# Scores of the first batch as one float32 product of whole keys and queries, with a new order of operations

## The chip, the core and the metric

The kernel runs on one core of a Trainium2 chip. The core has a matrix engine (TensorE, PE in the profile; its weight loads stand apart as PEld), a vector engine (VectorE, DVE), a scalar engine (ScalarE, ACT), a general engine (GpSimd, POOL) and a queue engine that issues transfers (SyncE, SP). Each works through its own list of instructions in a fixed order, and they wait for each other by semaphores. TensorE reads operands from SBUF and writes only to PSUM, whose eight banks are drained by the other engines. The metric is the device time of one execution in microseconds (us).

## The reference

Three layers follow one another. Four batches of eight heads, 576 positions and 64 numbers a head go through attention in which each query keeps its 32 highest scores; the result goes through a mixture of eight experts with one expert a token; and that through a layer with a softmax-weighted unit and a normalisation.

```python
scores = scale * np.matmul(q, k.transpose(0, 1, 3, 2))
kth = np.partition(scores, -top_k, axis=-1)[..., -top_k:-top_k + 1]   # top_k = 32
scores = np.where(scores >= kth, scores, -1e9)
attn = softmax(scores);  x = attn @ v                 # B, H, S, D = 4, 8, 576, 64
e_idx = np.argmax(x @ w_gate + modality_bias[modality_id], axis=1)
out[e_idx == e] = gate_w * (np.maximum(x @ w1[e], 0) @ w2[e])   # 8 experts, 512 -> 1024 -> 512
h = x @ w_in;  solu = h * softmax(h);  y = layer_norm(solu) * g_ln @ w_out   # 512 -> 1024 -> 512
```

## The kernel before, in words

**Attention.** A batch (b) has four pairs of heads (p) and five tiles of queries (t): four of 128 rows and a last one of 64. `prep_kv` loads the keys of a pair, turns them by TensorE into a PSUM bank and hands them to `parts_of`; `prep_q` does the same for the queries of a tile. `parts_of` (lines 530 to 533) makes two numbers of each float32 number: ScalarE copies the bank into the plane `hi` in the type float32r, which keeps fewer bits (L532), and VectorE takes the difference into the plane `lo` (L533). A pair of keys takes two such steps, one over 512 columns and one over 128; a query tile takes one over 512, the last tile of a batch two over 256.

`scores` (lines 609 to 633) then makes the scores of one tile and one pair, which the text calls a group of scores. It forms the product from three float32r terms, hi with hi, hi with lo and lo with hi, each in two halves of 288 columns, and for a full tile for the two heads of the pair: 3 x 2 x 2 = 12 matmuls (L628). The two heads lie in the two halves of the array's rows (64 rows each). For the last tile the two heads stand side by side in one operand, and a group has 3 x 2 = 6 matmuls over all 128 rows. A batch has 16 groups of 12 and 4 groups of 6.

From each group `unit` takes one head at a time (a unit): ScalarE copies the two halves out of PSUM (L649, L659), VectorE finds the 32nd highest score by rounds of maximum and replacement (L661 to L678), GpSimd and ScalarE mask and take the exponential (L689 to L693). There are 144 units. `pair` multiplies with the values (L722 to L771), and `route` and `place` pick each token's expert and scatter its row to a list in DRAM (L818 to L858).

**Statics.** The weights `w_in` and `w_out` of the last layer come as doubles and are brought into two float32r planes by ScalarE, GpSimd, VectorE (L386 to L390, L470) and TensorE (L408, L443). The first batch's units and this work run at the same time.

**Experts and the last layer.** When enough rows are listed, `front` picks the fullest expert (L915 to L920), gathers its rows (L933) and turns them (L960); `back` multiplies by `w1` (L1025) and `w2` (L1046) in float32; `moe2` runs the last layer (L1067, L1128) in float32r terms. A float32 matmul of the program shows as two matmuls in the trace: L1025 stands there x960 for 480 of the program.

**The order.** Every operation is a step (`Op`) of a generator. The table `ORDER` is a string of digits, one for each step: the digit says which of the generators that are ready goes next. The buffers (`TUNE`) and the priorities (`GET`) decide which generators are ready. So the string, not the chip, fixes the order of the instructions on every engine.

Of the kernel before, what the change touches and what calls it, by code (L numbers as in the profile page):

```python
# [8 lines left out]
F32 = mybir.dt.float32  # L9
# [9 lines left out]
NP = H // 2  # L19
# [20 lines left out]
    "0022556001111111222202334444441115555513333554455556663666440000011233434366666667777555622223377703344441"  # L40
    "1225663226045437747747406244166644451000031111111130400000411333300033442121332155132333044345113544003002"
    "2221556420644464341444401111133622511114446463624461162233636556444412225115552666643315111111814443333332"
    "6675575751944228611434436633667114411111133011114445411122543323522224400445222255336065046005555110432222"
    "2200005561700205223616333333302660022221146007728584472226901553333384557744446661633334115665656213333547"
    "6222677788111425113316778122311145366676522233011100660001230005544112222222225113501133400555600511222467"
    "3311111115525444000113230000230550034434441111111000520002222113355555667335733302112446666553550000388877"
    "7617999894446361111118002455511220050005777444710005350053344992201187472242665111145333133311461114466115"
    "5115688888823662244166661743233223355443434343345352234452222622116010011224443304678776434234311224005511"
    "1112234343320335500044435553226610055671534444521053153536744154224526332222112002244003335255333000002344"
    "4611751160131557833333323436522245334775677676271166114492534763247788222283226233334623225577777766445443"  # L50
    "3666661226222757564126542524655772333043333115055353400042255000400223323000000011154021200042224004443456"
    "78822224811334555258570007301637788822662aa887800653347844785761334521604111100225562266644123333000046551"
    "1160011662242344552772060044034011120001112242112466666601177777665654522756565558856765888403033331133223"
    "2013232224445501133365533446553366001828333378835558803335454572201322621224411111455666163322412221154577"
    "2331301122305533334240113355541224551111110231200332456700543432224677757747418776662661777741365774422545"
    "3313436111022000133232455000111133335689842321434337422667533115511377122222254506411333453666112222245613"
    "4461556663347250132886868954424444442445663316666561111556111777745110433226565116231234002005555554331311"
    "1111144443152244533545545774201000122335444461551111322205300233400001331200134332400002211167880000544440"
    "2427351115453300000001022686622222474748807877112328664441140343345527704500442522666600077826558868990114"
    "5950411555700007556555034220222004455116665771581118882882223444445502266665773225100011111165335455522506"  # L60
    "0000022153231232311333466661102224255664134221115544432422233033555517757000102667788655522111115544127774"
    "4552311111000555777772944664304707225241115866282735311441434334455599033554aa445519a555775589633ab9255989"
    "8266400511166711167353011115001948882555007420344773333115766565576778945636776785157012334799993388942145"
    "5457443333233324656311022244222344003422300400011116614544336115844113393225957556641110500022272554440024"
    "6776225666200117734300100044846781711665333316744411411300172722999a64466977177763333311177859a11b11113354"
    "4488558188991116626227000555142553677677622264405245663362222554223633302220456666661145451111220885772655"
    "8776340846a91446767567755555552711111334455551288544122467133233035536531424250111111333465541100533222511"
    "4456063121332337891884545413355555254454622233622224775663557223337751130511689377454333512442266171455411"
    "22222005550000007654445577722802633725588a2bb01668888748717457559a6699973334556674445997a339a9aa9991155333"
    "3888888955674444555116877179444424541118167111304331221134434344555602344894331312334433455015556651566666"  # L70
    "4522222222215454666342111000231114444006006612301344220011661111104266726634311111311232555464113342884855"
    "56a430115881a811776533122252666645657528311899555583331332831466899998811188bb3377871178787111974553999799"
    "a91572722244469999a66333388544b559966136794444014367676226356566539181115555114377311117222992542433555446"
    "46467464647161333728111116633552223322776655645415111656578444017658744a9999132222244255568343322224445544"
# [165 lines left out]
def attn_moe_solu_kernel(ctx, tc, q, k, v, mid, w_gate, mbias, w1, w2, w_in, w_out, g_ln, out):  # L240
# [1351 lines left out]
    c = 0  # L1592
# [77 lines left out]
```

## Time and profile before

| | |
|---|---|
| three timed runs | 952.91, 955.68, 955.14 us; median 955.14 us |
| profiled execution: its own time, its span | 952.62 us, 950.8 us |
| TensorE busy | 874.6 us |
| VectorE busy | 779.7 us |
| ScalarE, GpSimd busy | 670.9 us, 585.1 us |

The span runs from the first to the last instruction of the profiled execution; 1.8 us of its time lie around it. Busy time adds what an engine executes, without its waits. A matmul's recorded time contains its way through the array, so the spacing of a stream of matmuls is read from the starts in the timeline. A pair of units is under way from about 8 us on; the first expert's products start at 166 us, the last unit's scores end at about 754 us, and from there TensorE runs through the rest of the experts and the last layer.

### The profile page before, as it was taken

The page shows a single profiled execution, that of the slowest core. Times are in us where ns is not written, and L with a number is a line of the kernel's source. Part 1 is how long each engine was busy: PE and PEld are TensorE (multiplying, and loading weights), DVE is VectorE, ACT ScalarE, POOL GpSimd, SP SyncE. Part 2 cuts the span into 40 slices and gives each one's busy share as a digit, 9 for nine tenths or more (in the row PEclk, how much of TensorE's full clock was granted, in tenths as well). Part 3 has the DMA queues.
Part 4 walks back from the last instruction along what each step waited for, and adds up shares of the span by engine and source line. Part 5 has one row for each costly group of instructions (what it writes and reads, how often), then busy time and mean ns, then how long its engine had stood idle before and what let it go on. Part 6 is the DMA issues. An engine that isn't in the chain of part 4 may idle for free.

```text
span 950.8 us, 21544 instructions
## 1 busy us (share of the span) xinstructions
PE 874.6 (92%) x6830; PEld 730.7 (77%) x6830; DVE 779.7 (82%) x2444; ACT 670.9 (71%) x1698; POOL 585.1 (62%) x1352
## 2 busy tenths in 40 slices
PE   5766787989999999999999999999999999999994
PEld 3544455977888888879888888888887988889872
DVE  7998998999999999999999999999999943422320
ACT  3867876878787778878877788788778863633432
POOL 4677856657666767675677677666677666520222
PEclk9888887999999999999999999999999999999998
DMA  6624233444624343455243434443432337624000
GB/s 173 188 67 138 91 89 93 124 115 140 174 79 148 112 137 113 119 157 154 79 137 103 125 90 138 121 123 113 136 96 86 114 107 224 195 89 118 6 23 26
DMA packets 140952, 110.72 MB, mean 116 GB/s; under 512 B 47233, under 2 KB 116893, under 8 KB 140830
## 3 DMA queue, kind: packets, MB, share of 16 engines
q1 hardware_dynamic: 136478, 93.92, 34.4%
q0 software_dynamic: 4352, 15.34, 4.7%
q8 instruction: 56, 0.92, 0.4%
q14 instruction: 66, 0.54, 0.2%
HBM read 97.11 MB, written 12.13 MB: 115 GB/s over the span
## 4 chain that ended last, share of the span: by engine, by line
PE 50%; DVE 14%; POOL 10%; ACT 5%; issue 5%; DMA 2%; POOLq 0%; DVEq 0%; ACTq 0%
PE po L1128 7%; PE ph L1025 7%; PE py L1046 7%; PE ph L1067 6%; PE po L755 5%; PE pS L628 4%; PE pt L722 4%; DVE M L669 3%; POOL e L691 2%; PE py L1346 2%; PE ph L1326 2%; DVE tht L678 2%; DMA xg<-xlist,li 2%; PE pt L960 1%; PE px L765 1%
## 5 line engine op out<-in xcount | busy, mean ns | idle before, releaser
L691 POOL TENSOR_TENSOR e<-ss,e 128x576 f32<-128x576 f32 x144 | 206.3, 1434 | 55.4 <-ACT e L690 52.9
L693 ACT ACTIVATE e<-e,nb 128x576 f32<-128x576 f32 x144 | 112.0, 778 | 25.7 <-POOL e L691 24.7
L669 DVE MATCH_REPLACE8 M<-tops,M 128x288 f32<-128x288 f32 x288 | 127.4, 445 | 0.0
L1025 PE MATMUL ph<-xT,wraw 128*128 128x128 f32 x960 | 126.2, 278 | 1.1 <-DVE M L662 0.5
L1046 PE MATMUL py<-hh,wraw 128*128 128x128 f32 x960 | 125.8, 278 | 1.1 <-ACT hh L1030 1.1
L690 ACT ACTIVATE e<-ss,bt 128x576 f32<-128x576 f32 x144 | 111.5, 778 | 19.4 <-POOL bt L689 19.2
L1025 PEld LDWEIGHTS ph<-xT,wraw 128*128 128x128 f32 x960 | 115.4, 192 | 6.3 <-issue 3.1
L1046 PEld LDWEIGHTS py<-hh,wraw 128*128 128x128 f32 x960 | 115.3, 192 | 5.6 <-issue 2.7
L1128 PE MATMUL po<-wo,lT 128*128 128x512 f32 x432 | 112.0, 404 | 2.6 <-ACT lT L964 2.6
L1067 PE MATMUL ph<-wi,yT 128*128 128x512 f32 x432 | 110.2, 403 | 0.8 <-ACT ss L649 0.7
L755 PE MATMUL po<-eT,vt 128*64 128x128 f32 (+1 forms) x1600 | 104.7, 273 | 5.2 <-DVE qT L533 1.9
L678 DVE MAX8 tht<-M 128x8 f32<-128x576 f32 x144 | 108.1, 754 | 1.2
L628 PE MATMUL pS<-kT,qT 64*128 64x288 f32 (+1 forms) x864 | 94.4, 322 | 10.0 <-DVE xs L776 4.3
L755 PEld LDWEIGHTS po<-eT,vt 128*64 128x64 f32 x1600 | 84.6, 140 | 20.7 <-ACT eT L725 5.8
L1128 PEld LDWEIGHTS po<-wo,lT 128*128 128x128 f32 x432 | 77.6, 188 | 23.8 <-DVE lT L968 3.3
L1067 PEld LDWEIGHTS ph<-wi,yT 128*128 128x128 f32 x432 | 78.3, 188 | 19.8 <-issue 1.6
L628 PEld LDWEIGHTS pS<-kT,qT 64*128 64x128 f32 (+1 forms) x864 | 72.2, 193 | 27.0 <-issue 7.8
L725 ACT ACTIVATE eT<-pt 128x512 f32<-128x512 f32 x144 | 82.0, 597 | 10.4 <-PE pt L722 9.8
L722 PE MATMUL pt<-identr,e 128*128 128x128 f32 x576 | 85.0, 284 | 4.1 <-ACT e L693 1.7
L722 PEld LDWEIGHTS pt<-identr,e 128*128 128x128 f32 x576 | 68.8, 146 | 12.7 <-ACT e L693 3.5
L661 DVE TENSOR_TENSOR M<-pS,ss 128x288 f32<-128x288 f32 x144 | 64.7, 450 | 9.3 <-ACT ss L659 7.2
L689 POOL TENSOR_SCALAR bt<-tht 128x1 f32<-128x1 f32 x144 | 34.0, 236 | 62.2 <-DVE tht L678 51.7
(256 smaller groups left out, 1848.4 us busy)
## 6 DMA issues: line engine op xcount, KB each, us to landing
wraw<-in_moe_w_dram SPq DMA_DIRECT2D x256, 256.0 KB
kr<-in_k_dram SPq DMA_DIRECT2D x32, 128.0 KB
qr<-in_q_dram SPq DMA_DIRECT2D x16, 256.0 KB
raw<-in_moe_w_out_dram SPq DMA_DIRECT2D x8, 512.0 KB
vt<-in_v_dram SPq DMA_DIRECT2D x32, 128.0 KB
raw<-in_moe_w_in_dram SPq DMA_DIRECT2D x8, 512.0 KB
wstage<-da SPq DMA_DIRECT2D x8, 256.0 KB
wc<-wstage SPq DMA_DIRECT2D x8, 256.0 KB
```

Source lines behind the costliest of these rows:

```text
L628: nc.tensor.matmul(bank[s][hf], x[r, a, p, :], kt[r, c, at:at + HALF], start=i == 0, stop=i == 2)
L669: nc.vector.match_replace(out=M, in_to_replace=rounds[r], in_values=M, imm_value=NEG)
L678: t0 = yield Op("DVE", 660, lambda: nc.vector.max(th, W), deps=[t0, tm])
L690: yield Op("ACT", 667, lambda: nc.scalar.activation(e, ss, AF.Relu, bias=bt, scale=-BIG))
L691: yield Op("POOL", 1360, lambda: nc.gpsimd.tensor_tensor(e, ss, e, op=OP.subtract))
L693: yield Op("ACT", 760, lambda: nc.scalar.activation(e, e, AF.Exp, bias=nb, scale=0.125, accum_out=z))
L722: nc.tensor.transpose(pt[:, c, :], ef[:, at:at + 128], ident)
L755: nc.tensor.matmul(po[hs, :n], w, x, start=c == 0, stop=c == 4)
L1025: nc.tensor.matmul(ph[:, :n], w[:, kk * 128:(kk + 1) * 128], x[0][:, kk, :n], start=kk == 0, stop=kk == KD - 1)
L1046: nc.tensor.matmul(py[c // k_][:, c % k_, :], w[:, c * 128:(c + 1) * 128], hs[m], start=m == 0 and c % k_ == 0, stop=m == KF - 1 and c % k ...
L1067: nc.tensor.matmul(ph, y[a][:, kk, :], wi[b][:, kk, i * 512:(i + 1) * 512], start=kk == 0 and j == 0, stop=kk == KD - 1 and j == 2)
L1128: nc.tensor.matmul(po, l[a][:, c, :], wo[b][:, kk, :], start=kk == 0 and j == 0, stop=kk == KF - 1 and j == 2)
```

## The change

Batch 0 alone is computed in another way (`WHOLE = 1`). `parts_of` then makes one ScalarE copy in float32 into the plane `hi`, and the VectorE step into `lo` is not there. `scores` then forms one float32 product of the planes `hi`, in place of three float32r terms: 4 matmuls of the program for a full tile, 2 for the last one, with the same halves and the same rows of the array. Batches 1 to 3 are as before. The table `ORDER` is a new one over its whole length; a line of it stands in the diff.

```diff
 ORDER = (
-    "0022556001111111222202334444441115555513333554455556663666440000011233434366666666777555622223377703344441"
...
+    "0022556101101112343311114444444455554546666035544466624222393352575788846566777557777766669377882222223375"
...
-    def parts_of(hi, lo, pt, n):
-
+    WHOLE = 1
+
+    def parts_of(b, hi, lo, pt, n):
+
+        if b < WHOLE:
+            yield Op("ACT", 55 + n * 833 // 1000, lambda: nc.scalar.activation(hi.bitcast(F32), pt, AF.Copy))
+            return
         yield Op("ACT", 55 + n * 833 // 1000, lambda: nc.scalar.activation(hi, pt, AF.Copy))
         yield Op("DVE", 70 + n * 1042 // 1000, lambda: nc.vector.tensor_tensor(lo, pt, hi.bitcast(F32), op=OP.subtract))
...
         def mm():
-            for i, (a, c) in enumerate(((0, 0), (0, 1), (1, 0))):
+            terms, dt = (((0, 0),), F32) if b < WHOLE else (((0, 0), (0, 1), (1, 0)), F32R)
+            for i, (a, c) in enumerate(terms):
                 for hf in range(2):
                     for s in range(n // 64):
                         r = slice(64 * s, 64 * s + 64) if n == 128 else slice(0, 128)
                         at = 64 * (1 - s) + hf * HALF
-                        nc.tensor.matmul(bank[s][hf], x[r, a, p, :], kt[r, c, at:at + HALF], start=i == 0, stop=i == 2)
+                        nc.tensor.matmul(bank[s][hf], x[r, a, p, :].bitcast(dt), kt[r, c, at:at + HALF].bitcast(dt),
+                                         start=i == 0, stop=i == len(terms) - 1)
```

The lines behind the first part of the diff move by 5 to 7: L533 of before is L538 of the changed kernel, L628 is L634, L661 is L668, L669 is L676, L672 is L679, L915 is L922.

TensorE at the start of the program, before; `kr` and `qr` are raw keys and queries, `pS` the scores, `da` and `dc` pieces of a static weight:

```order
L563 MATMUL pt<-identr,kr 128x128 x4
L570 MATMUL pt<-identr,kr 128x64
L589 MATMUL pt<-identr,qr 128x128 x4
L628 MATMUL pS<-kT,qT 128x288 x12
L350 MATMUL pt<-identr,cs 128x64
L563 MATMUL pt<-identr,kr 128x128 x4
L570 MATMUL pt<-identr,kr 128x64
L589 MATMUL pt<-identr,qr 128x128 x4
L408 MATMUL pw<-da,identr 128x512
L408 MATMUL pw<-dc,identr 128x512
L443 MATMUL pm<-da,onesf 128x512
```

And the same place now:

```order
L568 MATMUL pt<-identr,kr 128x128 x4
L575 MATMUL pt<-identr,kr 128x64
L594 MATMUL pt<-identr,qr 128x128 x4
L350 MATMUL pt<-identr,cs 128x64
L634 MATMUL pS<-kT,qT 128x288 x4
L594 MATMUL pt<-identr,qr 128x128 x4
L568 MATMUL pt<-identr,kr 128x128 x4
L575 MATMUL pt<-identr,kr 128x64
L408 MATMUL pw<-da,identr 128x512
L634 MATMUL pS<-kT,qT 128x288 x4
L408 MATMUL pw<-dc,identr 128x512
```

The second query tile is turned before the second pair's keys, and the second group of scores stands between the pieces of the first static weight, where before it stood behind two static weights.

VectorE from its first instruction of attention, before; `ss` is a unit's copied half, `M` the larger of each two scores, `tops` the maxima found so far:

```order
L533 TENSOR_TENSOR kT<-pt,kT 128x512
L344 COPY iw<-identr 64x4x64 x2
L533 TENSOR_TENSOR kT<-pt,kT 128x2x64
L533 TENSOR_TENSOR qT<-pt,qT 128x512
L661 TENSOR_TENSOR M<-pS,ss 128x288
L662 TENSOR_TENSOR M<-pS,ss 128x288
L665 MAX tops<-M 128x8
L661 TENSOR_TENSOR M<-pS,ss 128x288
L662 TENSOR_TENSOR M<-pS,ss 128x288
L665 MAX tops<-M 128x8
```

And now:

```order
L344 COPY iw<-identr 64x4x64 x2
L668 TENSOR_TENSOR M<-pS,ss 128x288
L669 TENSOR_TENSOR M<-pS,ss 128x288
L672 MAX tops<-M 128x8
L676 MATCH_REPLACE M<-tops,M 128x288
L668 TENSOR_TENSOR M<-pS,ss 128x288
L669 TENSOR_TENSOR M<-pS,ss 128x288
L679 MAX tops<-M 128x8
L672 MAX tops<-M 128x8
```

Three differences of keys and queries are gone from the head of the list, and the first unit's first replacement stands ahead of the second unit.

VectorE around the first pick of an expert, before; `rk`, `pos` and `cq` belong to the routing of the tile ahead of it, `pmx` to the pick, `qT` here is the last query tile of batch 0:

```order
L852 SCALAR_TENSOR_TENSOR rk,pos<-rk,oh 128x8
L853 TENSOR_TENSOR cq<-cq,pc 128x8
L665 MAX tops<-M 128x8
L672 MAX tops<-M 128x8
L669 MATCH_REPLACE M<-tops,M 128x288
L470 TENSOR_TENSOR wo_101<-pw,wo_100 128x512 x2
L669 MATCH_REPLACE M<-tops,M 128x288
L672 MAX abt<-M 128x8
L533 TENSOR_TENSOR qT<-pt,qT 64x4x64 x2
L669 MATCH_REPLACE M<-abt,M 128x288
L672 MAX tops<-M 128x8
L707 RECIPROCAL rz<-z 128x2
```

And now:

```order
L859 SCALAR_TENSOR_TENSOR rk,pos<-rk,oh 128x8
L860 TENSOR_TENSOR cq<-cq,pc 128x8
L676 MATCH_REPLACE M<-tops,M 128x288
L685 MAX tht<-M 128x8
L679 MAX tops<-M 128x8
L714 RECIPROCAL rz<-z 128x2
L676 MATCH_REPLACE M<-tops,M 128x288
L922 MAX pmx<-pend 128x8
```

The two static differences (L470) and the two query differences (L533) are no longer between the routing and the pick. The pick itself was the 306th instruction of VectorE's list and is the 293rd, 13 instructions earlier.

## Rows read from the trace of the kernel before

**Rows 1.** Page, parts 1 and 2: span; TensorE's granted clock in 40 slices.

```profile
span 950.8 us, 21544 instructions
...
PEclk9888887999999999999999999999999999999998
```

**Rows 2.** Windows by stage: stretch, length, busy time (instructions) by engine, clock, DMA share, GB/s.

```profile
0.00:25.00 25.00, 14.68 (x55) 8.36 (x56) 17.52 (x50) 10.21 (x22) 10.71 (x30) 1.00 0.68 175
25.00:125.00 100.00, 70.84 (x391) 43.84 (x389) 94.99 (x247) 76.34 (x175) 77.32 (x96) 0.85 0.37 112
125.00:163.50 38.50, 31.71 (x190) 21.97 (x191) 35.16 (x110) 26.16 (x65) 22.87 (x51) 0.81 0.38 112
163.50:250.00 86.50, 82.81 (x766) 71.41 (x766) 83.56 (x277) 70.58 (x188) 57.69 (x152) 1.00 0.48 134
250.00:750.00 500.00, 490.27 (x4277) 426.87 (x4276) 476.40 (x1554) 398.22 (x1042) 337.92 (x821) 1.00 0.41 119
750.00:900.00 150.00, 148.40 (x1004) 131.18 (x1003) 61.02 (x187) 73.54 (x182) 64.02 (x168) 1.00 0.40 123
```

**Rows 3.** Chain of waits, 100 to 180 us: start, length, engine, tile, line.

```profile
125.87 1.74 PE pS L628 x9
...
133.94 6.37 PE pw L408 x19
...
145.42 0.99 PE pS L628 x12
...
150.40 0.33 DVE qT L533
...
151.16 0.44 DVE qT L533
...
158.62 5.53 DMA xg<-xlist,li
...
166.15 1.98 PE ph L1025 x16
```

**Rows 4.** Line 533 up to 152 us: count, min/median/max ns, first to last start.

```profile
L533 DVE TENSOR_TENSOR kT<-pt,kT x8: 278/482/692, 6.1 to 35.7; 128x512 fp32r<-128x512 f32 x4, 128x128 fp32r<-128x128 f32 x4
L533 DVE TENSOR_TENSOR qT<-pt,qT x6: 397/669/692, 7.9 to 151.2; 128x512 fp32r<-128x512 f32 x4, 64x256 fp32r<-64x256 f32 x2
```

**Rows 5.** Window up to 152 us, line 533 alone: VectorE's busy time.

```profile
0.00:152.00 152.00, 7.06 (x14) 0.89 0.41 119
```

**Rows 6.** Waits of all engines up to 163.5 us: total, times, longest.

```profile
PE pt L563 <- DMA kr<-in_k_dram: 11.1, 3, 4.4
```

**Rows 7.** Line 628 up to 163.5 us: TensorE's score matmuls.

```profile
L628 PE MATMUL pS<-kT,qT x168: 285/394/607, 7.9 to 162.0; 64*128 64x288 f32 x168
```

**Rows 8.** TensorE's timeline, 340 to 375 us: start, length, line, form, count.

```profile
351.99 1.95 PE L1025 MATMUL ph<-xT,wraw 128*128 128x128 f32 x16
353.78 0.41 PE L765 MATMUL px<-iw,oT 128*128 128x144 f32 x2
...
362.73 1.07 PE L628 MATMUL pS<-kT,qT 64*128 64x288 f32 x12
363.73 0.66 PE L722 MATMUL pt<-identr,e 128*128 128x128 f32 x4
...
368.96 1.31 PE L755 MATMUL po<-eT,vt 128*64 128x128 f32 x20
370.20 3.06 PE L1128 MATMUL po<-wo,lT 128*128 128x512 f32 x12
373.10 0.41 PE L765 MATMUL px<-iw,oT 128*128 128x144 f32 x2
```

**Rows 9.** Groups by form: weight loads in float32 (L1025) and float32r (L628).

```profile
L1025 PEld LDWEIGHTS ph<-xT,wraw 128*128 128x128 f32 x960 | 115.4, 192 | 6.3 <-issue 3.1 <-DVE M L662 0.7 <-DVE xs L835 0.6
...
L628 PEld LDWEIGHTS pS<-kT,qT 64*128 64x128 f32 x768 | 58.9, 194 | 26.0 <-issue 7.6 <-ACT eT L725 4.7 <-DVE xs L776 4.5
```

More of the change, by code (lines that the diff above doesn't have):

```diff
@@ L39 @@
 ORDER = (
[L40 to L74, printed above, removed]
@@ new lines @@
+    "8884455266003455331143345688777275881117722422222222275543577778885664427722227773443666666434334477783155"
+    "5555727245122222456555772945577222226688376674744477773366255554833333333355522776378882442399655588686432"
+    "6666423388976133052522035530221330000103315445524220511222113532200225444556666006623700711656302214534422"
+    "6431668301441181114446156333172622322122333386678513118844236344522277377555555332448471111443666677775277"
+    "2352274711113433545457111121234156666882227722221110024420022222204415511133440011453544522050015662112111"
@@ L95 @@
+    "5555255341344446440075061115522224000144000444444322211112222000111202232233112222003335114112001011014220"
+    "0223010110002230221551334454330301344000000033133440301000000000000000000000000000001123330110012222222222"
+    "2333330011222233222220111110110002111300001033222100110200121000111111221111100300000111100111000111112002"
+    "21200000000000"
 )
@@ L565, in prep_kv @@
         yield Op("PE", 440, tr)
-        yield from parts_of(kt[:, 0, 64:576], kt[:, 1, 64:576], pt.rearrange("p c n -> p (c n)"), 512)
+        yield from parts_of(b, kt[:, 0, 64:576], kt[:, 1, 64:576], pt.rearrange("p c n -> p (c n)"), 512)
         yield "put", ("B", 1)
@@ L572, in prep_kv @@
         ends = kt.rearrange("p a (e n) -> p a e n", n=64)[:, :, 0:10:9, :]
-        yield from parts_of(ends[:, 0], ends[:, 1], bc(pl, 2, 1), 128)
+        yield from parts_of(b, ends[:, 0], ends[:, 1], bc(pl, 2, 1), 128)
         yield "put", ("B", 1)
@@ L593, in prep_q @@
         if n == 128:
-            yield from parts_of(x[:, 0], x[:, 1], pt, NP * n)
+            yield from parts_of(b, x[:, 0], x[:, 1], pt, NP * n)
         else:
@@ L602, in prep_q @@
                 r = slice(64 * s, 64 * s + 64)
-                yield from parts_of(x[r, 0, :, r], x[r, 1, :, r], pt[r], NP * n)
+                yield from parts_of(b, x[r, 0, :, r], x[r, 1, :, r], pt[r], NP * n)
         yield "put", ("B", 1)
```

65 lines of the change are left out of this document (45 added, 20 removed).

## The prediction

> **What bounds the kernel now.** I read the windows by stage first [rows 2]. The reader is to see two regimes. From 163.5 to 900 us TensorE is busy 82.81 + 490.27 + 148.40 = 721.5 of 736.5 us, all of it at the full clock: it is the bound, and only 15.0 us are idle. Up to 163.5 us it is busy 14.68 + 70.84 + 31.71 = 117.2 us and idle 46.3, with a granted clock of 0.85 and 0.81 in two of the three windows. VectorE, in contrast, is busy 94.99 + 35.16 = 130.2 of the 138.5 us between 25 and 163.5: it bounds this first stretch. The page's clock row says the same: digits below 9 stand in the first slices and the last one alone [rows 1].
>
> Then I read the chain of waits around the seam [rows 3]. Between 125 and 146 us it runs on TensorE (a group of scores of 1.74 us at the low clock, 6.37 us of static products, another group of 0.99 us). Then it goes through VectorE, where two query differences of L533 (0.33 and 0.44 us) stand on it themselves, to the gather of the first expert's rows (5.53 us) and to the first expert's products at 166.15 us. So the time is, roughly, the moment at which TensorE becomes dense plus the work that is left for it by then. The change can move the moment, through VectorE, and the work, through the products. I costed both, and then asked what the new order may do.
>
> **What VectorE loses.** In batch 0 the differences of L533 go: up to 152 us the line has 8 instructions for keys (four over 512 columns, four over 128) and 6 for queries (four over 512, two over 256) [rows 4], 14 in all, which are the whole of batch 0. Together they keep VectorE busy 7.06 us [rows 5]. All lie ahead of the first gather, in the stretch that VectorE bounds, so the first term is -7.06 us at most. The first pick moves up by 13 instructions in VectorE's list where 14 are removed, so the new order puts hardly any other work in their place.
>
> Not all of it need arrive. The differences of the keys of pairs 2 to 4 start by 35.7 us, while TensorE waits 11.1 us in three waits for the raw keys [rows 6]. Work that is saved in front of an arrival is not saved after it. A difference over 512 columns takes about 0.68 us and one over 128 about 0.28 (the kinds on either side of the median of 482 ns), so three pairs make 2.9 us. Bounds of the loss are 0 and 2.9. I take 1.0, nearer to nothing, because VectorE idles only 5.0 us between 25 and 125 us [rows 2]: it has static weights to convert meanwhile.
>
> ScalarE's copies stay in number and size, and write another type. I cost them at nothing; ScalarE is busy 76.34 of 100 us in the second window [rows 2], which would hide some tenths. The bank of the turned keys is handed back one VectorE step earlier; I count no gain for it.
>
> **What TensorE gains in work.** Before, a full group takes 1.00 us for 12 matmuls (362.73 to 363.73) [rows 8]. The two heads must be running side by side there, in the two halves of the array: a float32r matmul of 512 columns takes 2.90 / 12 = 0.242 us (370.20 to 373.10) [rows 8], which is 0.136 for 288 columns; six pairs at that price make 0.82 us, and 0.18 are left for filling and draining. Twelve in a row would make 1.63.
>
> A float32 matmul is not shown with 64 rows and 288 columns. From the nearest rows: 16 float32 instructions of 128 columns take 1.79 us (351.99 to 353.78), 0.112 each, two for a matmul of the program [rows 8]. For 288 columns that is 0.252, so a group has 8 instructions, in pairs 4 x 0.252 = 1.01, with the 0.18 it is 1.19 us: +0.19. Float32 instructions do run side by side in halves of the array's columns, 20 in 1.24 us (368.96 to 370.20), 0.062 each [rows 8]; halves of the rows have no float32 row. The price lies between 1.01 (+0.01, nothing to fill) and 8 x 0.252 + 0.18 = 2.20 (+1.20, nothing side by side). I take +0.19, since the pairs of L755 and those of L628 both overlap. A group of the last tile has 6 matmuls over all rows, which become 4 instructions: the same passes and the same +0.19.
>
> Where do they fall? Up to 163.5 us there are 168 score matmuls, 14 groups of 12 [rows 7]; the other two full groups and the four of the last tile come in the dense part, which makes 6 x 0.19 = 1.1 us. Of the 14, two stand on the chain: the one at 145 us (+0.19) and the one at 126 us, which ran at the low clock and costs twice that (+0.4). The other twelve, 2.3 us, are covered by TensorE's 46.3 idle us; if that cover failed they would cost those 2.3. The second term is +1.7 us.
>
> The Trainium skill has a rule that speaks against this change. The loads of weights in float32 take 192 ns in the trace (L1025) and those in float32r 194 (L628) [rows 9]: no difference. "TensorE: Matmul & The Clock Gate", section "Weight-path perf modes — Fast Weight Load (FWL) and DoubleRow", says that the fast way of loading weights is off for float32 and makes loads about twice as quick where it is on. By the rule, eight loads at twice the present spacing of 1.00 / 12 us would pace a group at 1.33 us instead of 1.19, an estimate from that page, and the six dense groups and the two on the chain would add about 1.3 us to the sum. By the rows they add nothing, and the sum goes by the rows.
>
> **The order.** Its price has no row. Macroscopically the lists look alike: on TensorE the same transposes of keys and queries open the program, with the second group of scores some entries earlier. What an order can win or lose in the dense part is bounded by its idle 15.0 us there [rows 2]: it can win no more than these, and I take a third, 5 us, as a fair gain, half as much again, 7.5 us, as a fair loss, and 0 as the value.
>
> **The sum.** -7.06 + 1.0 + 1.7 + 0 = -4.4 us. The profiled execution took 952.62 us, 1.8 more than its span of 950.8 [rows 1], and would take 948.2. It stands 2.5 us below the median of the runs shown, 955.14; from the median the same step gives 950.7 us, and that is the forecast.
>
> **The rivals.** *No change.* The end of the first stretch is set by the arrival of keys and by the static products at 134 us, so that only what VectorE saves behind the keys counts: two query differences of about 0.67 and two of about 0.4 us, 2.1. For it speak the 11.1 us of waits for keys and the 20 us of the chain on TensorE [rows 3, 6]; against it, that the static products wait for static weights which VectorE itself converts. It gives -2.1 + 1.7 = -0.4, 954.7 us.
>
> *Slower: the heads' float32 products do not run side by side.* The place is the group of scores, the price +1.20 us for a full one. The two in the dense part give 2.4, the four of the last tile 0.8, that at 145 us 1.2, that at 126 us at the low clock 2.4, together 6.8; of the twelve others' 14.4 us I let a quarter through, 3.6. The sum is -7.06 + 1.0 + 6.8 + 3.6 = +4.3, 959.4 us. It decides once the extra exceeds the 6.1 us that VectorE brings, when some six pairs in ten run one after the other. For it speaks that no row has such a product; against it, both kinds of pairs that do overlap [rows 8].
>
> *Slower: the new order.* Its dense part has half as many waits again: +7.5, so +3.1 and 958.2 us. For it speaks that this table is new over its whole length, and 15.0 idle us in 736.5 are little to start from; against it, that the picks keep their places.
>
> **How the numbers follow.** The forecast has 0.55, no change 0.20, the products 0.10, the order 0.15. What a measurement of this kernel can tell from no change is 0.3%, 2.9 us, so faster means below 952.3 and slower above 958.0. The forecast's own range is 946.5 to 953; 0.48 of its 0.55 lies below 952.3, and 0.05 comes from the lower edge of no change: faster 0.53. The rest of these two, 0.07 and 0.14, with 0.04 from the order's better half, makes no change 0.25. The products and the rest of the order leave 0.22 for slower. The range reaches from a fair gain by the order, 950.7 - 5, to the order's loss: 945.5 to 958.5.
>
> **What would show it.** The first expert's products should start near 161 us instead of 166. VectorE's busy time up to there should fall by about 7 us, with its share unchanged. A full group of batch 0 should take about 1.2 us at the full clock, with its matmuls starting two by two. TensorE's idle time after the seam should stay near 15 us. A group above 1.8 us would speak for the products; a start at 165 us or later for no change; a start at 161 us with more than 20 idle us behind it for the order. An end well below 946 us would say that the order gains, which I do not count on.

## The result and the profile after

The changed kernel took 943.68 us (median of 4 runs, 943.18 to 947.95), against 955.0 us for the kernel before in runs beside it (median of 4, 952.91 to 955.68). The ratio is 0.9895, with a 95% interval of 0.9863 to 0.9927: about 10 us faster. A later measurement of the same two kernels (e4, below) gave 0.9887. The forecast was 950.7 us with a range down to 945.5, so the direction was right, and the gain is more than twice the 4.4 us that the sum had.

The profiled execution is the lowest of the four: 943.18 us, with a span of 941.4. That of the kernel before took 952.62, which is 2.4 below its median. So the two traces differ by 9.4 us.

The windows of the changed kernel, in the stretches of [rows 2]:

```profile
0.00:25.00 25.00, 15.79 (x54) 8.22 (x56) 16.79 (x55) 12.76 (x28) 11.71 (x33) 1.00 0.66 164
25.00:125.00 100.00, 74.32 (x363) 41.25 (x359) 93.28 (x243) 76.86 (x177) 80.43 (x98) 0.83 0.41 118
125.00:163.50 38.50, 32.14 (x213) 22.25 (x212) 36.83 (x114) 27.73 (x71) 22.88 (x53) 0.91 0.37 107
163.50:250.00 86.50, 84.12 (x764) 72.08 (x764) 82.34 (x280) 70.42 (x188) 59.03 (x155) 1.00 0.51 145
250.00:750.00 500.00, 492.68 (x4274) 428.60 (x4271) 476.82 (x1559) 400.48 (x1046) 337.08 (x819) 1.00 0.41 118
750.00:900.00 150.00, 147.52 (x978) 130.72 (x978) 56.55 (x166) 67.55 (x168) 62.95 (x169) 1.00 0.40 121
```

The reader is to see two things. In the third window TensorE executes 213 matmuls instead of 190 at a clock of 0.91 instead of 0.81: the dense part begins inside it, not behind it. And in the three dense windows TensorE is busy 724.3 of 736.5 us, so 12.2 are idle where 15.0 were.

Fixed stretches blur this, because the seam (the first expert's first product) has moved. So here are two windows of each kernel, first of before, then of after: up to the seam, and from the same place near the end on (the transposes and nine first products of the last layer behind the last float32 expert) to the last matmul:

```profile
0.00:166.10 166.10, 119.66 (x661) 76.05 (x661) 150.26 (x413) 115.29 (x267) 112.17 (x182) 0.87 0.41 120
...
900.00:939.20 39.20, 35.84 (x159) 27.10 (x157) 11.06 (x23) 15.17 (x28) 13.60 (x37) 1.00 0.06 21
```

```profile
0.00:160.90 160.90, 119.64 (x604) 69.16 (x604) 144.30 (x400) 115.06 (x267) 112.59 (x179) 0.87 0.44 124
...
893.20:929.60 36.40, 34.58 (x158) 27.05 (x156) 10.34 (x21) 14.71 (x27) 11.70 (x30) 1.00 0.06 23
```

The seam comes 5.2 us earlier. VectorE is busy 5.96 us less up to it, with 13 instructions fewer, and its share hardly changes: 90.5%, then 89.7%. Behind the seam the kernel before needed 773.1 us to its last matmul and the changed one 768.7 (929.6 - 160.9), 4.4 us less. In the last stretch TensorE does the same work (159 and 158 matmuls) in 36.4 us instead of 39.2: it idles 1.8 us in place of 3.4, and is recorded busy 34.58 us in place of 35.84.

The chain of waits of the changed kernel around the seam, the counterpart of [rows 3]:

```profile
121.70 2.22 PE pS L634 x8
...
130.62 4.43 PE pw L408 x14
...
140.31 1.17 PE pS L634 x8
...
146.16 0.17 DVE pmx L922
...
154.30 2.22 PE pS L634 x8
...
161.00 1.98 PE ph L1032 x16
```

The query differences are gone from it, and so is the gather: behind the pick at 146.16 the chain runs through VectorE's and TensorE's own work for the units. A float32 group of scores shows 2.22 us at the low clock (0.50 is granted in those two stretches, 1.2 GHz) and 1.17 at the full one.

### The profile page after: what moved, and what is told of

Read it like the earlier page. It is cut to its first block, busy times and chain, and to the rows that moved or that the text cites. A ratio compares the mean times of both kernels' runs of the same rounds, so it can differ in the third digit from the quotient of the medians.

```text
span 941.4 us, 21332 instructions
## 1 busy us (share of the span) xinstructions
PE 874.4 (93%) x6758; PEld 724.7 (77%) x6758; DVE 771.6 (82%) x2430; ACT 669.4 (71%) x1698; POOL 585.8 (62%) x1352
## 4 chain that ended last, share of the span: by engine, by line
PE 66%; DVE 10%; POOL 8%; ACT 5%; issue 3%; DMA 1%; POOLq 0%; SPq 0%; DVEq 0%; ACTq 0%
PE ph L1074 9%; PE ph L1032 9%; PE py L1053 9%; PE po L1135 7%; PE po L762 7%; PE pS L634 6%; PE pt L729 5%; POOL e L698 3%; DVE M L676 2%; PE py L1353 2%; PE ph L1333 2%; PE px L772 2%; PE pw L408 2%; PE pt L967 2%; DVE tht L685 1%
## 5 line engine op out<-in xcount | busy, mean ns | idle before, releaser
L1053 PE MATMUL py<-hh,wraw 128*128 128x128 f32 x960 | 128.0, 280 | 0.5 <-ACT hh L1037 0.5
L676 DVE MATCH_REPLACE8 M<-tops,M 128x288 f32<-128x288 f32 x288 | 127.3, 445 | 0.0
L700 ACT ACTIVATE e<-e,nb 128x576 f32<-128x576 f32 x144 | 112.1, 778 | 19.9 <-POOL e L698 18.5
L1053 PEld LDWEIGHTS py<-hh,wraw 128*128 128x128 f32 x960 | 117.2, 194 | 5.7 <-issue 3.8
L762 PE MATMUL po<-eT,vt 128*64 128x128 f32 (+1 forms) x1600 | 101.8, 270 | 2.5 <-ACT eT L732 1.5
L634 PE MATMUL pS<-kT,qT 64*128 64x288 f32 (+1 forms) x792 | 95.2, 342 | 6.7 <-DVE xs L783 3.9
L762 PEld LDWEIGHTS po<-eT,vt 128*64 128x64 f32 x1600 | 82.4, 138 | 19.9 <-ACT eT L732 4.7
L732 ACT ACTIVATE eT<-pt 128x512 f32<-128x512 f32 x144 | 82.7, 601 | 14.9 <-PE pt L729 13.4
L634 PEld LDWEIGHTS pS<-kT,qT 64*128 64x128 f32 (+1 forms) x792 | 67.2, 190 | 26.5 <-issue 6.0
L668 DVE TENSOR_TENSOR M<-pS,ss 128x288 f32<-128x288 f32 x144 | 64.8, 450 | 11.8 <-ACT ss L666 10.4
L656 ACT ACTIVATE ss<-pS 128x288 f32<-128x288 f32 x144 | 57.8, 410 | 15.5 <-PE pS L634 13.7
```

Of the source, the lines that this page charges most:

```text
L634: nc.tensor.matmul(bank[s][hf], x[r, a, p, :].bitcast(dt), kt[r, c, at:at + HALF].bitcast(dt), start=i == 0, stop=i == len(terms) - 1)
L676: nc.vector.match_replace(out=M, in_to_replace=rounds[r], in_values=M, imm_value=NEG)
L700: yield Op("ACT", 760, lambda: nc.scalar.activation(e, e, AF.Exp, bias=nb, scale=0.125, accum_out=z))
L762: nc.tensor.matmul(po[hs, :n], w, x, start=c == 0, stop=c == 4)
L1053: nc.tensor.matmul(py[c // k_][:, c % k_, :], w[:, c * 128:(c + 1) * 128], hs[m], start=m == 0 and c % k_ == 0, stop=m == KF - 1 and c % k ...
```

## The experiments

Two things were changed at once: the arithmetic (differences gone, one float32 product) and the table that sets the order. The theory of the prediction was that the arithmetic carries the gain and that the order is worth about nothing; its rival, after the result, that the order carries most of it. To tell them apart, an order was carried over exactly: the sequence in which one table places its steps was recorded, and a table was written that places the steps of the other kernel in the same sequence, with the 14 differences taken out, or put in right behind their ScalarE copies. Unless said otherwise no other step changes its place.

All ratios are to the kernel before, measured beside them (its medians were 955.53, 956.02 and 954.77 us in the three sets of runs). A ratio difference of 0.1% is 0.95 us.

| run | arithmetic | order | median us | ratio, 95% interval |
|---|---|---|---|---|
| e1 | new | old | 953.19 | 0.9974 (0.9958 to 0.9990) |
| e2 | old | new | 948.97 | 0.9919 (0.9888 to 0.9950) |
| e3 | new | new, old from the wide expert (L1333) on | 946.82 | 0.9904 (0.9882 to 0.9927) |
| e4 | new | new (the changed kernel again) | 944.75 | 0.9887 (0.9865 to 0.9909) |
| e5 | new | old up to the seam, then new | 947.99 | 0.9931 (0.9905 to 0.9958) |
| e6 | new | new up to the seam, then old | 947.45 | 0.9915 (0.9894 to 0.9936) |
| e7 | new | new up to about 39 us, then old | 952.81 | 0.9974 (0.9959 to 0.9990) |
| e8 | no differences, three products | old | 950.83 | 0.9949 (0.9933 to 0.9966) |
| e9 | differences kept, float32 product | old | 955.42 | 1.0011 (0.9994 to 1.0028) |
| e10 | no differences, three products | new | 942.83 | 0.9872 (0.9847 to 0.9896) |
| e11 | new | new up to about 99 us, then old | 949.07 | 0.9936 (0.9913 to 0.9958) |
| e12 | new, in batches 0 and 1 | new | 944.33 | 0.9888 (0.9865 to 0.9912) |

### Arithmetic and order apart: e1 to e4

e1 is the changed kernel with a table that keeps the old sequence (the first line of it):

```diff
 ORDER = (
-    "0022556101101112343311114444444455554546666035544466624222393352575788846566777557777766669377882222223375"
+    "0022556001111112220234444441115555513333554455556663666440000123434366666667777555622223377703344441256632"
```

> The new arithmetic of batch 0, with every remaining operation in the order of the kernel before (only the 14 differences are missing from it). Theory A, the order is the part that I mis-sized: the arithmetic alone gives what the sum said, 4 to 6 us, so about 950 us beside 955, the first expert's products near 161 us and TensorE idle about 18 us from there to its end. Theory B, the arithmetic gives everything: 944 us, idle time behind the seam 14 us or less. Theory C, each order fits only its own arithmetic: 953 us or more.

e2 is the kernel before with a table that has the new sequence:

```diff
 ORDER = (
-    "0022556001111111222202334444441115555513333554455556663666440000011233434366666667777555622223377703344441"
+    "0022556101101111223443311114444444455454546666035544466624222233933525757888465667775577777666693377882222"
```

> The arithmetic of the kernel before, with every operation in the order of the changed kernel (each of the 14 differences stands right behind its copy on ScalarE). Theory A: the order alone gives 4 to 6 us, about 950 us beside 955, first expert's products near 166 us, idle behind the seam about 14 us. Theory B: 955 us. Theory C: slower than before, 957 us or more.

e3 is the changed kernel in which the last 4.6% of the steps stand in the old sequence, from the first product of the wide expert on (L1333, 448 columns in float32r; it starts at 818.7 us). e4 is the changed kernel unaltered.

> The changed kernel up to the first matmul of the last large expert (4.6% of the operations are left then), and from there the remaining operations in the order of the kernel before. In the traces the changed kernel gains 2.7 us behind that point. Theory A in its narrow form, the tail's order is worth these: 2 to 3 us slower than the changed kernel. Rival: the tail only follows what the earlier part left, and the time stays within 1 us of the changed kernel.

> The changed kernel itself beside the others on the same chip, as the mark for e1 to e3. By its four runs so far 943 to 948 us, 11 us below before; if the gap to before here were 5 us, what was left unexplained would be scatter between runs and no order.

The new arithmetic in the old order is 0.26% faster than before, 2.5 us. The new order with the old arithmetic is 0.81% faster, 7.7 us. With both it is 1.13%, 10.8 us. So the order is worth 7.7 us with the old arithmetic and 0.87%, 8.3 us, with the new one (e1 to e4; the intervals are far apart). The theory that the order is worth nothing falls. Of the expectations for e1 none holds as written: the time lies where theory C had it, but by C's reason e2 would have been slower than before, and it is 7.7 us faster; theory A had the arithmetic at 4 to 6 us, and it gave 2.5. For e2 and e3 theory A came true (949 us; 2.1 us behind e4 by the medians).

e1 and the changed kernel execute the same work up to the seam, so their traces can say where the order gains there. The window up to the seam of e1, to be read beside that of after above:

```profile
0.00:169.00 169.00, 126.03 (x604) 73.17 (x604) 144.87 (x399) 115.33 (x267) 112.49 (x182) 0.86 0.41 118
```

Both have 604 matmuls, 399 or 400 VectorE instructions of 144.87 or 144.30 us and 267 ScalarE instructions; but e1 arrives 8.1 us later. VectorE idles 24.1 us in e1 and 16.6 after. One pair of traces is not enough here, though: e5 (below) has the same lists as e1 up to the seam and arrives at 166.5. So here are the traces of all kernels but e12, by the order and the differences that they have. The idle time is the start of the first expert's products less VectorE's busy time up to there:

| order up to the seam | differences of batch 0 | traces | first expert's products start, us | VectorE idle up to there, us |
|---|---|---|---|---|
| old | kept | before, e9 | 166.1, 170.0 | 15.8, 18.7 |
| old | gone | e1, e5, e8 | 169.0, 166.5, 165.8 | 24.1, 21.2, 21.9 |
| new to 39 or 99 us, then old | gone | e7, e11 | 167.4, 166.2 | 23.0, 22.2 |
| new | gone | changed, e3, e4, e6, e10 | 160.9, 161.9, 160.6, 163.1, 160.7 | 16.6, 17.8, 16.6, 18.5, 16.8 |
| new | kept | e2 | 167.4 | 14.7 |

Equal lists lie up to 2.5 us apart. Beyond this scatter, with the differences gone, VectorE idles about 5 us less in the new order and the seam comes 5 to 6 us earlier. With the differences kept the traces show no earlier seam in the new order; what of e2's 7.7 us lies ahead of the seam stays open (the trace of before ran 2.4 us below its median, that of e2 1.2 above).

What VectorE waits for up to 160 us (total, times, longest), in e1 and then in the changed kernel:

```profile
DVE M L668 <- ACT ss L666: 11.6, 4, 7.2
DVE rz L714 <- POOL z L713: 2.5, 3, 1.7
DVE dd L386 <- POOL dd L385: 2.5, 4, 1.0
DVE xs L842 <- POOL se L841: 1.2, 1, 1.2
DVE lg L825 <- ACT xs L778: 1.0, 2, 0.7
```

```profile
DVE M L668 <- ACT ss L666: 7.7, 3, 7.1
DVE dd L386 <- POOL dd L385: 2.9, 5, 1.4
```

The wait of 7.1 to 7.2 us is the one for the first scores at all. Before the change, the first differences of keys and queries stood inside this stretch; without them VectorE simply waits for the copied scores. The waits at `rz` (the reciprocals of the softmax's sums), `xs` and `lg` (two steps of the routing), 4.7 us together, are not among those of the changed kernel. They stand in every trace with the differences gone and the old order from 39 us on (e1, e5, e7 and e8: 4.5 to 4.9 us) and in no trace with the new order up to the seam. The second wait for scores is longest in e1. TensorE in e1, from the end of the second tile's transposes (start, length, line, tile, form, count):

```profile
15.23 1.11 PE L594 MATMUL pt<-identr,qr 128*128 128x128 f32 x4
16.40 2.04 PE L408 MATMUL pw<-da,identr 128*128 128x512 f32 x2
...
22.75 1.42 PE L408 MATMUL pw<-dc,identr 128*128 128x512 f32 x1
24.09 2.19 PE L634 MATMUL pS<-kT,qT 64*128 64x288 f32 x8
```

and the same in the changed kernel:

```profile
16.47 2.07 PE L408 MATMUL pw<-da,identr 128*128 128x512 f32 x2
18.47 1.36 PE L634 MATMUL pS<-kT,qT 64*128 64x288 f32 x8
```

In e1 the second group of scores stands behind the two static weights and begins at 24.09; VectorE, which is through with the first group at 22.93, waits 3.83 us for it:

```profile
21.52 1.41 DVE L685 MAX8 tht<-M 128x8 f32<-128x576 f32 x2
26.76 0.46 DVE L668 TENSOR_TENSOR M<-pS,ss 128x288 f32<-128x288 f32 x1 [3.83 <-ACT ss L666]
```

In the changed kernel it begins at 18.47, between them, and this wait is not there. But e5, with the lists of e1, has its second group at 21.98 and waits only 0.76 us (TensorE, then VectorE):

```profile
21.98 1.24 PE L634 MATMUL pS<-kT,qT 64*128 64x288 f32 x8
```

```profile
23.69 0.46 DVE L668 TENSOR_TENSOR M<-pS,ss 128x288 f32<-128x288 f32 x1 [0.76 <-ACT ss L666]
```

In e8, which has the same order with three products, it waits 3.12 us. What the order saves at this place changes from execution to execution, and no single pair of traces prices it.

At the end lies the other piece that can be named. TensorE's last products in the changed kernel and in the kernel before (the times in brackets are idle time and what ended it):

```profile
909.73 2.96 PE L1135 MATMUL po<-wo,lT 128*128 128x512 f32 x12
...
914.36 2.96 PE L1135 MATMUL po<-wo,lT 128*128 128x512 f32 x12
...
918.89 0.66 PE L967 MATMUL pt<-identr,u 128*128 128x128 f32 x4 [1.13 <-DVE u L1091]
919.30 5.85 PE L1135 MATMUL po<-wo,lT 128*128 128x512 f32 x24
...
926.27 3.33 PE L1135 MATMUL po<-wo,lT 128*128 128x512 f32 x12 [0.69 <-ACT lT L971]
```

```profile
921.85 0.66 PE L960 MATMUL pt<-identr,u 128*128 128x128 f32 x4 [0.75 <-DVE u L1084]
923.20 3.32 PE L1128 MATMUL po<-wo,lT 128*128 128x512 f32 x12 [0.69 <-ACT lT L964]
...
928.60 6.13 PE L1128 MATMUL po<-wo,lT 128*128 128x512 f32 x24 [1.21 <-ACT lT L964]
...
935.85 3.33 PE L1128 MATMUL po<-wo,lT 128*128 128x512 f32 x12 [0.69 <-ACT lT L964]
```

In the old order, three of the last output products wait for ScalarE's copy of their turned operand (0.69, 1.21, 0.69 us). In the new one they are spread so that other products stand before two of them, and one wait of 0.69 is left, beside one of 1.13 for VectorE where before had 0.75. TensorE's idle time falls by 1.5 us. The rest of the gain does not show as idle time: twelve products are recorded with 2.96 us in a stream and with 3.32 behind a wait. e3, with the old end, has the waits of before again (0.75, 0.69, 1.20, 0.69) and is 0.17%, 1.6 us, behind the changed kernel. The intervals of e3 and e4 overlap, but the traces are clear about the end. From the start of the wide expert's first product to that of the last product of all pass 113.4 to 114.0 us in the eight kernels with the old end (before, e1, e3, e6, e7, e8, e9, e11) and 110.5 to 110.6 in the six with the new one (changed, e2, e4, e5, e10, e12): the end is worth 2.9 us, with either arithmetic.

### Where the order gains: e5, e6, e7 and e11

Four kernels with the new arithmetic change from one sequence to the other at a place: at the first expert's first product (e5, e6), at the fourth group of scores (e7), at the ninth (e11). The edit is again the table; for e7, against e1, the first two lines, and from the third on all are alike:

```diff
-    "0022556001111112220234444441115555513333554455556663666440000123434366666667777555622223377703344441256632"
-    "2604543774774740624416664445100031111111304000004113333000334421213321551323330443451135440030022221556420"
+    "0022556101101112343311114444444455554546666035544466624222393352575788846566777557777766669377882222223375"
+    "8884455266003455331143345688777275881117722422222222275543577778885664427722221011551445115443022221556420"
```

> New arithmetic; the operations up to the first expert's first product in the order of before, everything behind it in the new order. Theory A, the order gains in two places, the first stretch and behind it: this one has only the second part, 3 to 4.5 us better than the same arithmetic in the old order throughout (953.2), about 949 to 950 us, with TensorE's last product ending some 769 us behind the first expert's as in the changed kernel. Rival, all of the order's gain lies in the first stretch: 952 to 953 us.

> New arithmetic; the new order up to the first expert's first product, the order of before behind it. Theory A: the first expert's products near 161 us as in the changed kernel, and 772 us from there to the last product as in the kernel before: 948 to 949 us. Rival, all in the first stretch: 944 to 945 us. Rival, nothing in the first stretch: 952 to 953 us.

> New arithmetic; the new order only up to the fourth group of scores (about 39 us, 3% of the operations), then the order of before. In the old order with the new arithmetic VectorE waits 3.8 us at 26.8 us for the second group of scores, which stands behind the products of two static weights on TensorE; in the new order it does not wait there. Theory H, this head is what lets the missing differences be worth something: 3 to 4 us better than the old order throughout (953.2), about 949 to 950 us, first expert's products 4 us earlier than its 169.0. Rival, the waits come back later in the stretch: 952 to 953 us.

> New arithmetic; the new order up to the ninth group of scores (about 99 us in the changed kernel, 9% of the operations), then the order of before. The new order up to 39 us alone gave 0.4 us, up to 161 us 5.7 us. Theory, the gain builds up along the stretch, in the pieces where VectorE no longer waits for GpSimd and ScalarE's static weights: 949 to 951 us. Rival, it lies in the last part, the static products and the first pick from 99 to 161 us: 952 to 953 us.

Against e1 (0.9974), the new order up to 39 us brings nothing (e7, 0.9974), up to 99 us 0.38%, 3.6 us (e11), up to the seam 0.59%, 5.6 us (e6). The new order behind the seam alone brings 0.43%, 4.1 us (e5). The intervals of e6 and e1 lie apart; those of e5 and of e11 touch that of e1. The two parts, 5.6 and 4.1, come to 9.7 where the whole order brings 8.3, so within the intervals they add up, and the part behind the seam is worth 2.7 us (8.3 - 5.6) to 4.1. The end's 2.9 us fill this. In the dense part between, from the first expert's products to the wide expert's, the traces show no gain by the order: 656.5 to 659.3 us in the old one, 655.4 to 658.2 in the new one, with TensorE idle 11.8 to 14.9 and 11.4 to 14.4 us.

e11 came where its theory had it, e5 and e6 up to a microsecond below theirs, and e6 started its first expert at 163.1 and not near 161.

e7 was a miss that teaches. It has the second group of scores early and waits 0.74 us for it, against 3.83 in e1 and 0.76 in e5; yet its time is that of e1. VectorE's waits in e7 up to 160 us:

```profile
DVE M L668 <- ACT ss L666: 8.6, 4, 7.0
DVE dd L386 <- POOL dd L385: 4.2, 5, 1.0
DVE rz L714 <- POOL z L713: 2.8, 2, 2.4
DVE xs L842 <- POOL se L841: 1.2, 1, 1.2
DVE lg L825 <- ACT xs L778: 0.9, 2, 0.6
```

The waits at `rz`, `xs` and `lg` are all still there, and VectorE idles 23.0 us up to the seam, as with the old order. In e11 the wait at `rz` is gone and the two others stand. Beside e1, the 3.0 us fewer at the scores stand against 1.7 more for GpSimd's step of the static weights (L385) and 0.3 more at `rz`. GpSimd in turn waits there for ScalarE. Between 38 and 100 us this is 3.9 to 5.0 us in e1, e5 and e8, and 0.2 to 2.0 in the kernels that have the new order to 99 us or farther. The line in e7 and in the changed kernel:

```profile
POOL dd L385 <- ACT dd L383: 7.9, 5, 2.4
```

```profile
POOL dd L385 <- ACT dd L383: 2.0, 2, 1.8
```

So nothing is gained by the head alone, and the gain comes with the orders that go on to place the steps behind it otherwise (e11, e6). That it comes by the static steps, and by the waits at `rz`, `xs` and `lg`, is a reading of traces; no run changed these steps alone.

### The two halves of the arithmetic: e8, e9, e10 and e12

e8 takes the differences away and keeps three float32r products: of the high plane with itself, three times, so that the low parts are left out of batch 0's scores. The order is the old one. e10 is the same in the new order.

```diff
-            yield Op("ACT", 55 + n * 833 // 1000, lambda: nc.scalar.activation(hi.bitcast(F32), pt, AF.Copy))
+            yield Op("ACT", 55 + n * 833 // 1000, lambda: nc.scalar.activation(hi, pt, AF.Copy))
...
-            terms, dt = (((0, 0),), F32) if b < WHOLE else (((0, 0), (0, 1), (1, 0)), F32R)
+            terms, dt = ((0, 0),) * 3 if b < WHOLE else ((0, 0), (0, 1), (1, 0)), F32R
```

> Order of before without the 14 differences; the scores of batch 0 keep three float32r terms, each formed from the high planes, so the low parts are left out of them and TensorE has the work of the kernel before. Theory W, what VectorE saves falls into waits for the keys and the scores: 952 to 954 us, VectorE's idle time up to the first expert's products 6 us or more above the 15.8 of before. Rival P, VectorE's saving arrives and the dearer products of batch 0 eat it: 949 us or less, seam 6 us earlier than in the kernel before.

> New order, without the differences, batch 0's scores as three float32r terms of the high planes (the low parts are left out of them). Beside the old arithmetic in the new order (949.0) it lacks only VectorE's 7 us; beside the changed kernel (944.75) it has the cheaper products. Theory F, the new order lets VectorE's saving through: 942 to 943 us, 6 to 7 us below the former and about 2 below the latter. Rival, the saving is worth 5 us or less in any order: 944 to 945 us.

e9 makes the float32 product but keeps the 14 differences, in the table of before:

```diff
             yield Op("ACT", 55 + n * 833 // 1000, lambda: nc.scalar.activation(hi.bitcast(F32), pt, AF.Copy))
+            yield Op("DVE", 70 + n * 1042 // 1000, lambda: nc.vector.tensor_tensor(lo, pt, hi.bitcast(F32), op=OP.subtract))
             return
```

> Order of before, all 14 differences kept (they give zeros that nobody reads), and batch 0's scores as one float32 product. The arms so far put the price of the products at 953.2 - 950.8 = 2.4 us in this order. If the prices add up: 958 us, 2 to 3 us above before. Rival, the products cost only where VectorE waits for them: 956 us, no change.

e12 computes batch 1 in the new way as well, in the new order without batch 1's 14 differences (4 of the other steps had to move):

```diff
-    WHOLE = 1
+    WHOLE = 2
```

> The changed kernel with batch 1 treated as batch 0 (14 differences fewer, 20 groups of scores as one float32 product; the rest in the new order). Its groups lie behind the seam, where TensorE is the bound and a group costs 1.17 instead of 0.99 us. Theory, what TensorE pays counts there and VectorE's saving does not: 20 x 0.18 = 3.6 us more, 947 to 949 us. Rival, VectorE bounds the units there too and its 7 us count: 941 us or less.

Without the differences the kernel gains 0.51%, 4.9 us, in the old order (e8 to before) and 0.47%, 4.5 us, in the new one (e2 to e10). The float32 product costs 0.25%, 2.4 us, in the old order (e8 to e1), 0.15%, 1.4 us, in the new one (e10 to e4, whose intervals overlap), and 0.11%, 1.0 us, with the differences kept (e9, whose interval holds no change). The order is worth 0.77%, 7.4 us, between e8 and e10, a third figure that agrees with 7.7 and 8.3. The gain without the differences is clear of its interval in the old order, and in the new one the two intervals just overlap. Each price of the product is no larger than the intervals around it; that all three have one sign is what bears the reading. So each half is worth about the same in either order.

Of the expectations, e8's 950.8 us lies between its two theories, and e9 is its rival's case, no change. e10 has the 942.8 us of theory F, but the step to it from e2 is 4.5 us by the ratios, which is its rival's 5 us or less in any order. e12 lies between its theory and its rival.

e12 has the time of the changed kernel. Its window from the seam to the start of the wide expert, and that of the changed kernel:

```profile
161.30:818.40 657.10, 648.22 (x5510) 558.36 (x5507) 587.71 (x1942) 509.16 (x1331) 442.30 (x1102) 1.00 0.44 128
```

```profile
160.90:818.60 657.70, 645.53 (x5580) 560.84 (x5579) 592.81 (x1956) 509.18 (x1331) 443.22 (x1102) 1.00 0.44 128
```

TensorE works 2.7 us more (3.6 were expected) and idles 8.9 instead of 12.2. VectorE is relieved of 5.1. In these two traces the products' cost is paid in the dense part, and about as much of TensorE's idle time goes; the two cancel. That the idle time goes because VectorE has less to do was not tested apart.

No kernel that computes the whole scores beats the changed one by more than its interval.

## Why the prediction was wrong

**Which step failed.** It is the one on the order: "what an order can win or lose in the dense part is bounded by its idle 15.0 us there", "and 0 as the value". The order is worth 7.4 to 8.3 us, in three pairs of runs with different arithmetic. That is more than the gap of 6.4 us between the sum of 4.4 and the 10.8 measured in e4, since the arithmetic brought less than its sum. The step looked at the stretch from 163.5 to 900 us alone, and there the value of 0 was about right: the dense part takes as long in either order. The gain lies on both sides of it. Ahead of the seam it is 5.6 us with the new arithmetic (e6), where the 15.8 us for which VectorE idles before were not looked at as something that an order can take away. Behind 900 us it is 2.9, where the last products wait. That the "fair gain" of 5 us is near what the new order brings behind the seam (2.7 to 4.1 us) is luck: it was a third of the idle time of a stretch in which nothing was gained. And "Macroscopically the lists look alike" was concluded from the head of one list; the difference named there, the second group of scores "some entries earlier", is worth nothing by itself (e7).

**VectorE's loss of 7.06 us, less 1.0 for the keys' arrival.** The sum had -6.1; the runs have -4.9 (e8) and -4.5 (e10). The mechanism was right, and the size somewhat off: bounds of 0 and 2.9 were set on what would not arrive, and 2.2 to 2.6 did not. The prediction looked for the loss at the keys of pairs 2 to 4. The traces show most of what did not arrive at the first scores, which come no earlier. VectorE's first step on them starts at 10.24 us before and, without the three differences that had stood ahead of it, at 10.30 in e8; by the prediction's own lengths these three are 1.6 us:

```profile
10.24 0.46 DVE L661 TENSOR_TENSOR M<-pS,ss 128x288 f32<-128x288 f32 x1 [1.67 <-ACT ss L659]
```

```profile
10.30 0.46 DVE L668 TENSOR_TENSOR M<-pS,ss 128x288 f32<-128x288 f32 x1 [6.77 <-ACT ss L666]
```

**The products, +1.7 us.** Measured +2.4, +1.4 and, with the differences kept, +1.0. The price of a group was right, though a third group stands on the chain (154.30, 2.22 us) where two were counted. The changed kernel's timeline at the full clock (start, length, line, tile, form, count) has a full group, the first group of a last tile and what follows each:

```profile
167.72 1.24 PE L634 MATMUL pS<-kT,qT 64*128 64x288 f32 x8
168.89 1.31 PE L762 MATMUL po<-eT,vt 128*64 128x128 f32 x20
...
184.01 1.14 PE L634 MATMUL pS<-kT,qT 128*128 128x288 f32 x4
184.99 0.60 PE L568 MATMUL pt<-identr,kr 128*128 128x128 f32 x4
```

A full group takes 1.17 us, where 1.19 was worked out and before it was 1.00 [rows 8]; the last tile's takes 0.98. The heads run side by side, so the rival of products in a row (2.20) is out.

The Trainium skill, in "TensorE: Matmul & The Clock Gate", section "Weight-path perf modes — Fast Weight Load (FWL) and DoubleRow", has float32 weights load without the fast way; by that rule, with float32r on the fast side, which the page does not say, the prediction's estimate of a group was 1.33 us. The trace disagrees: 1.17. Loads of score weights in float32 take about what those in float32r took (194 ns, [rows 9]). Those of the six float32 groups behind the seam, in the changed kernel (count, min/median/max ns, first to last start, forms):

```profile
L634 PEld LDWEIGHTS pS<-kT,qT x32: 182/187/192, 167.7 to 194.1; 64*128 64x128 f32 x16, 128*128 128x128 f32 x16
```

**The whole arithmetic.** -4.4 in the sum, -2.5 (e1) and -3.1 (e2 to e4) in the runs. The sum had both terms too favourable: what VectorE loses (4.5 to 4.9 us and not 6.1) and, in the old order, the products (2.4 and not 1.7). Taken alone the arithmetic is hardly more than a measurement of this kernel can tell from no change.

**What the prediction said it would show.** The start of the first expert at 161 us came true (161.00), and so did VectorE's 6 us less with an unchanged share. The busy time is the arithmetic's (144.87 us in e1 too), but the seam and the share are not its signs: e1, with all of the arithmetic, starts the expert at 169.0 with VectorE's share at 144.87 / 169.0 = 85.7%, and e5 at 166.5. In the traces the seam is near 161 only where the differences are gone and the order is new; e2, with the new order alone, has it at 167.4. The timed runs show no such dependence: there the two are worth about the same with and without each other. TensorE's idle time from the first expert's products to the wide expert's fell to 12.2 us instead of staying near 15 (14.9 before), but that is no sign of the order: e1 has 12.6. The sentence that held the explanation was the last: "An end well below 946 us would say that the order gains".

**The rivals.** No change was wrong for the kernel, though e1, 2.5 us below before, is close to what it would have been without the new table. The slower ones did not happen.

## What to carry to other kernels

A change that comes with a new order is two changes, and the order of the same instructions can be worth more than the edit (here 8 us of 955, against 3 for the arithmetic). Before an order is priced at zero, look at the waits of the engine that bounds each stretch, at the program's head and end as well as in its dense part, and ask for each one whether the new lists put what it waits for earlier; the sum of these waits is a first estimate of the most that an order can win there. A wait that is removed at one place is no gain yet (e7): what follows it can wait instead. And one trace can show a wait that the next trace of the same lists does not have (3.83 us in e1, 0.76 in e5), so a reading is worth checking against every trace at hand that shares the lists.

## What was not expected of the hardware

The float32 products with 64 rows overlap in pairs as the float32r ones do: eight instructions in 1.17 us at the full clock and in 2.22 us at the low one (a granted clock of 0.50), which no row of before had shown. The four of a last tile, which go through all rows one behind the other, take 0.98 us, so eight in a row would take about twice that.
